# A spectral filter and a snake MLP on one core: the first DFT stage of batches 3 to 7 folded on GpSimd, and one inverse piece moved

## The chip, the cores and the metric

The kernel runs on one core of a Trainium2 chip. The metric is device time in microseconds (us) of one execution, the median over several runs; lower is better. A profiled execution of the same program gives the page and the trace that are quoted here. Its own time is not the median of the runs, and both are given below.

The engines are named as the profile names them: PE (TensorE, matrix products; PEld is its weight load), DVE (VectorE), ACT (ScalarE), POOL (GpSimd) and SP (SyncE, which here does nothing but issue DMAs). Each engine takes its instructions in the order in which the program emits them.

## The reference, cut to what matters

```python
batch, seq, dim = (8, 3008, 256)             # x; filt_r, filt_i: (1505, 256)
n_tokens, d_model, d_ff = (24064, 256, 2048) # w_in (256, 2048), w_out (2048, 256), alpha (2048,)

X = np.fft.rfft(x, axis=1)
Y = X * (filt_r + 1j * filt_i)[None, :, :]
y = np.fft.irfft(Y, n=x.shape[1], axis=1)    # per batch and channel, 3008 long

h = y.reshape(8 * 3008, 256) @ w_in
s = np.sin(alpha * h)
g = h + s * s / (alpha + 1e-09)
out = g @ w_out
```

## The kernel before

**The mixing.** A length of 3008 is 47 x 64. The transform over 3008 is made in two stages of matrix products in float16: a first stage over 47 points (of its 47 frequencies 24 are enough, since the input is real), and a second over 64 points with the twiddle factors in its tables. The way back is two stages too. For batches 1 to 7 a class `Spectral` (line 164) holds the pieces of one batch:

- `load_x` (line 175, DMA issue on line 141, queue of POOL) brings one of four quarters of the batch, 94 rows of 8 x 256, and casts it to float16.
- `first` (line 178) is one of 16 pieces of the first stage: one product of a 94 x 96 table `wf_t` with 512 columns (line 181) into a PSUM tile of the pool `fps`, which has two buffers, and a copy of it to `t1_h` by `evac`. After every fourth piece SP issues a store of the quarter to a DRAM tile `d1` (line 186).
- `load_t2` (line 189, DMA on line 193, POOL's queue) reads `d1` back with other axes on the partitions, in four groups `g` of two DMAs. It waits for the stores of `d1`.
- `forward` (line 196, products on line 201), `product` (line 211) and `cross` (line 219) make the second stage and multiply by the filter; line 208 swaps two halves of the partitions by DMA through SP. There are 12 pieces `u`; piece `u` needs group `u // 3` of `load_t2`.
- `inverse` (line 224, products on line 232) is the way back over 64 points, 12 pieces; every third piece SP stores a group to a DRAM tile `d2` (line 239). `load_t4` (line 242, SP) reads it back, and `last` (line 247, products on line 254) is the way back over 47 points, 16 pieces, into `y`.

Batch 0 has a path of its own (lines 267 to 507) ahead of the main loop and is not touched by the change, except for where two of its tiles are allocated.

**The MLP.** The 24064 columns of `y` are cut into 48 chunks, twelve for two batches: eleven of 512 columns and one of 384. `hidden` (line 534) makes one block of 128 hidden units for a chunk: two products of 512 columns (line 541) into one of four PSUM tiles, a sine on ACT (line 545) and the snake's sum on DVE (line 546), which leaves its mark in `marks["snake"]`. `project` (line 550) makes half of the second product for 128 columns: eight products of 256 columns (line 558); ACT copies two results at a time (line 566) and `store` (line 576) writes them out, from chunk 5 on through SP alone (line 586), in up to eight DMAs of a group.

**The order.** `tc.manual_schedule()` keeps the order in which the program emits. The main loop (line 640) runs in steps, eight to a chunk. A step emits two `hidden` (four products of 512), then the mixing pieces that are due (`slot(step)`), then one `project` of the chunk before (eight products of 256), then what is due by `slot(step + 0.5)`. What is due when is written out by hand in lines 602 to 623: `put(at, fn, ...)` gives a piece its step. `z = 48 * b` is where a batch's own chunks begin. `slot` emits at most one piece that has products (`pe=True`) in each half step, unless it is over a step late; a piece that has to stay behind holds back all that is due after it.

**`evac`** (line 157) gives two of three copies out of PSUM to ACT and one to DVE, in turn.

**A wait written out**: `after(ins, marks["snake"])` in `load_x` (line 152) lets a load start only when the last snake sum emitted so far is done.

Of the kernel before, what the change touches and what calls it, by code (L numbers as in the profile page):

```python
# [9 lines left out]
FP16 = mybir.dt.float16  # L10
FP32 = mybir.dt.float32
# [11 lines left out]
NR = 2 * N1  # L23
NK = 4 * NS
FUSED = 1


def dft_tables():

    n1, n2 = np.arange(N1), np.arange(N2)  # L30
    s, q = np.arange(NS), np.arange(NQ)
    ph = 2 * np.pi * np.outer(n1, s) / N1
    w = np.stack([np.cos(ph), -np.sin(ph)], 1)
    wf = np.zeros((N1, 2, 2, NS, 2))
# [12 lines left out]
    d[0, :, :, 0] = c.transpose(0, 2, 1)  # L47
    d[1, :, :, 0] = sn.transpose(0, 2, 1)
    d[0, :, :, 1] = (-sn * sg).transpose(0, 2, 1)
    d[1, :, :, 1] = (c * sg).transpose(0, 2, 1)  # L50
    f16 = np.float16
    wf, wi = wf.reshape(N1 * 2, 2, NS, 2), 2 * wi.reshape(2, NS, 2, NR)
    wf0, wi0 = np.zeros((96, 2, 2, 32)), np.zeros((2, 2, 32, NR))
    wf0[:NR, :, :, :NS] = wf.transpose(0, 1, 3, 2)
    wi0[:, :, :NS] = wi.transpose(0, 2, 1, 3)
    d = d.reshape(128, NS, 128).astype(f16)
    e = d.transpose(2, 1, 0) * f16(0.125)
    return (wf.reshape(NR, NK).astype(f16), wi.reshape(NK, NR).astype(f16), d,
            wf0.reshape(96, 128).astype(f16), wi0.reshape(128, NR).astype(f16), e)


# [1 line left out]
def kernel(  # L63
# [8 lines left out]
    out: bass.AP,  # L72
):
    nc = tc.nc
    wf_host, wi_host, d_host, wf0_host, wi0_host, e_host = dft_tables()
    wf_dram = nc.inline_tensor(wf_host, name="wf_tbl")
    wi_dram = nc.inline_tensor(wi_host, name="wi_tbl")
    d_dram = nc.inline_tensor(d_host, name="d_tbl")
    wf0_dram = nc.inline_tensor(wf0_host, name="wf0_tbl")
    wi0_dram = nc.inline_tensor(wi0_host, name="wi0_tbl")  # L80
# [13 lines left out]
        return ctx.enter_context(tc.tile_pool(name=name, bufs=bufs, **kw))  # L94

    cpool = pool("consts", 1)
    xpool = pool("xp", 4)
    t2pool = pool("t2", 4)
    xfpool = pool("xf", 3)
    ppool = pool("pp", 4)  # L100
# [19 lines left out]
    y = cpool.tile([128, 2, 2, 32, NR], FP16)  # L120
# [15 lines left out]
    marks = {}  # L136

    def load_x(b, ch):
        xt = xpool.tile([NR, 8, C], FP16, name=f"x_{b}_{ch}", tag="x")
        for n0, n in [(0, 8)] if b or ch < 3 else [(0, 4), (4, 4)]:  # L140
            ins = nc.gpsimd.dma_start(  # L141
                out=xt[:, n0:n0 + n],
                in_=bass.AP(tensor=x.tensor, offset=x.offset + (b * S + ch * 8 + n0) * C,
                            ap=[[32 * C, NR], [C, n], [1, C]]),
            )
        if b == 0:
            marks["x", ch] = ins
        if b == 1:
            marks["x1", ch] = ins
            after(ins, marks["w_out"])  # L150
        if b > 1:
            after(ins, marks["snake"])
        return xt
# [3 lines left out]
    def evac(dst, src, on_act=None):  # L157
# [3 lines left out]
        else:  # L161
            marks["dve"] = nc.vector.tensor_copy(out=dst, in_=src)  # L162

    class Spectral:

        def __init__(self, b):
            self.b = b
            self.d1 = dpool.tile([2 * NS, N2, C], FP16, name=f"d1_{b}", tag="d1")
            self.d2 = dpool.tile([2 * NS, N2, C], FP16, name=f"d2_{b}", tag="d2")
            self.d1_rows = self.d1.rearrange("a (h n) c -> (a h) n c", h=2)  # L170
            self.d2_rows = self.d2.rearrange("a (h n) c -> (a h) n c", h=2)
            self.x, self.t2, self.t4, self.xf, self.xs, self.p = {}, {}, {}, {}, {}, {}
            self.fused = b >= FUSED

        def load_x(self, ch):
# [2 lines left out]
        def first(self, i):  # L178
            ch, j = divmod(i, 4)
            ps = fps.tile([128, 512], FP32, name=f"pa_{self.b}_{i}", tag="f")  # L180
            marks["pe"] = nc.tensor.matmul(out=ps[0:NK, :], lhsT=wf_t, rhs=self.x[ch][:, 2 * j:2 * j + 2, :],  # L181
                                           start=True, stop=True)
            r0 = 8 * (ch % 2)
            evac(t1_h[ch // 2][0:NK, r0 + 2 * j:r0 + 2 * j + 2, :], ps[0:NK, :])
            if j == 3:
                nc.sync.dma_start(out=self.d1_rows[:, 8 * ch:8 * ch + 8, :], 
                                  in_=t1_h[ch // 2][0:NK, r0:r0 + 8, :])
# [76 lines left out]
    id32 = cpool.tile([16, 16], FP32)  # L264
    nc.scalar.dma_start(out=id32, in_=id32_dram.ap())

    x0 = [xpool.tile([NR, 8, C], FP16, name="x_0_0", tag="x")] + [load_x(0, ch) for ch in range(1, 4)]
# [169 lines left out]

    def product_0(i):
        hc, w = blocks[i]
        p0[i] = xpool.tile([128, 2, 4, 128], FP16, name=f"p_0_{i}", tag="x")  # L440
        marks["products"] = nc.vector.tensor_tensor(
            out=p0[i].rearrange("p f s (k c) -> p f s k c", k=2),
            in0=xf0[i].rearrange("p s (k c) -> p s k c", k=2)[:, None].to_broadcast([128, 2, 4, 2, 64]),
            in1=filt_t[:, :, 4 * w:4 * w + 4].rearrange("p f s (k c) -> p f s k c", k=2)[..., 64 * hc:64 * hc + 64],
            op=ALU.mult)
# [148 lines left out]
    def put(at, fn, *args, pe=False):  # L594
        pending.append((at, len(pending), pe, fn, args))
# [6 lines left out]
    for b in range(1, B):  # L602
        s = s1 if b == 1 else Spectral(b)
        z = 48 * b
        if b > 1:
            for ch in range(4):
                put(22 + 4 * ch if b == 2 else z - 92 + 7 * ch, s.load_x, ch)
        for i in range(16):
            put(6.9 + 0.35 * i if b == 1 else 37 + 0.63 * i if b == 2 else z - 67 + 0.66 * i, s.first, i, pe=True)
        for g in range(4):  # L610
            put(12.5 if b == 1 else 47 if b == 2 else z - 56, s.load_t2, g)
        for u in range(12):
            inv = 23.5 + 1.25 * u if b == 1 else 59 + 2.1 * u if b == 2 else z - 40.8 + 2.3 * u
            fwd = inv - (6 if b == 1 else 6)
# [68 lines left out]
```

## Time and profile before

| | us |
|---|---|
| runs, median of 3 (lowest to highest) | 784.37 (783.44 to 784.44) |
| the profiled execution, its own time | 784.61 |
| its span, first to last instruction | 782.8 |

| engine | busy us | share of the span | instructions |
|---|---|---|---|
| PE | 771.7 | 99% | 5799 |
| DVE | 654.4 | 84% | 1165 |
| ACT | 617.0 | 79% | 1211 |
| POOL | 113.3 | 14% | 190 |

The span leaves 1.8 us of the execution's time outside the first and last instruction. An engine's busy time is the union of its instructions' times. PE overlaps its products: one of 512 columns is shown as lasting some 380 ns, but the next starts 216 to 220 ns after it, so the distance between starts, not the duration, is what a product costs. The profile's time line shows those starts. "x4" in it stands for four instructions in a row.

### The profile page before, as it was taken

Reading aid. Unit: us, or ns where it says so; the run is one execution under the profiler, and the core shown is the slowest. Engines: PE = TensorE matmul, PEld = TensorE weight load, DVE = VectorE, ACT = ScalarE, POOL = GpSimd, SP = SyncE. Lnnn points to the kernel's source line nnn. Section 1 sums busy time; section 2 is a strip of 40 time slices with the busy share of each in tenths; the row PEclk is TensorE's granted clock in tenths of the full one; section 3 lists DMA queues with packets and bytes.
Section 4 is the critical chain, followed back from the end, with each engine's and each line's share of the span. In section 5 each row is a group of like instructions: output and inputs, shape, how many; then the busy total and the mean of one; then the engine's idle time right before and its main releaser. Section 6 shows DMA issues by size and latency. Waiting matters only on the chain.

```text
span 782.8 us, 16640 instructions
## 1 busy us (share of the span) xinstructions
PE 771.7 (99%) x5799; PEld 535.3 (68%) x5799; DVE 654.4 (84%) x1165; ACT 617.0 (79%) x1211; POOL 113.3 (14%) x190
## 2 busy tenths in 40 slices
PE   8999999999999999999999999999999999999998
PEld 4757767676667766777666776767667776766666
DVE  7887997899879997899878998789977899777773
ACT  5797988888778887888878888788887887777674
POOL 6366444300020000200020000200002000000000
PEclk9999999999999999999999999999999999999999
DMA  9966676655654446645574454835456233421111
GB/s 217 269 121 165 130 161 200 150 128 118 192 143 99 121 109 188 154 119 105 133 210 105 104 122 128 227 82 129 106 157 180 66 98 80 118 62 28 41 41 54
DMA packets 86655, 100.99 MB, mean 129 GB/s; under 512 B 14896, under 2 KB 74294, under 8 KB 86572
## 3 DMA queue, kind: packets, MB, share of 16 engines
q1 hardware_dynamic: 74644, 71.11, 32.6%
q0 software_dynamic: 11712, 28.78, 18.7%
q8 instruction: 45, 0.74, 0.4%
q14 instruction: 38, 0.31, 0.2%
q10 hardware_dynamic: 216, 0.05, 0.0%
HBM read 55.72 MB, written 46.66 MB: 131 GB/s over the span
## 4 chain that ended last, share of the span: by engine, by line
PE 93%; DVE 2%; POOL 1%; ACT 1%; DMA 1%; issue 1%; SPq 0%; ACTq 0%; POOLq 0%; DVEq 0%
PE po L558 41%; PE ph L541 40%; PE pa L181 3%; PE pd L254 2%; PE pb L201 2%; PE pc L232 2%; POOL w L514 1%; PE pc L453 1%; DMA al<-in_moe_alpha_dram 1%; DVE v L546 1%; PE warm L377 1%; PE pb L431 1%; SPq L586 0%; POOL w L482 0%; PE pa L399 0%
## 5 line engine op out<-in xcount | busy, mean ns | idle before, releaser
L546 DVE SCALAR_TENSOR_TENSOR v<-cos_all,ph 128x512 f16<-128x512 f32 (+1 forms) x768 | 483.2, 672 | 108.3 <-ACT cos_all L545 104.3
L545 ACT ACTIVATE cos_all<-ph 128x512 f32<-128x512 f32 (+1 forms) x768 | 411.4, 592 | 95.6 <-PE ph L541 94.7
L541 PE MATMUL ph<-y,w 128*128 128x512 f16 (+1 forms) x1536 | 388.0, 374 | 1.5 <-DVE y L162 0.8
L558 PE MATMUL po<-w,v 128*128 128x256 f16 x3008 | 389.5, 272 | 0.0
L558 PEld LDWEIGHTS <-v 128*128 128x128 f16 x3008 | 288.3, 98 | 77.8 <-issue 1.5
L541 PEld LDWEIGHTS <-w 128*128 128x128 f16 x1536 | 147.9, 98 | 104.3 <-issue 3.8
L566 ACT COPY o<-po 128x512 f32<-128x512 f32 (+1 forms) x97 | 55.7, 574 | 20.6 <-PE po L558 14.0
L586 POOL DMA_DIRECT2D out_dram<-o x67 | 35.0, 530 | 206.4 <-ACT o L566 206.2
L193 POOL DMA_DIRECT2D t<-d x56 | 36.4, 662 | 171.0 <-DMA out_dram<-o 163.6
L204 ACT CAST xf<-pb 128x512 f16<-128x512 f32 x84 | 50.0, 595 | 12.6 <-PE pb L201 11.2
L141 POOL DMA_DIRECT2D x<-in_x_dram x32 | 17.2, 540 | 269.1 <-PE pc L232 159.9
L160 ACT CAST t_h<-pa 96x512 f16<-96x512 f32 x75 | 43.9, 585 | 9.0 <-PE pa L181 8.7
L160 ACT CAST y<-pd 128x376 f16<-128x376 f32 (+1 forms) x83 | 39.9, 481 | 8.1 <-PE pd L254 4.4
L254 PEld LDWEIGHTS <-t_a 96*128 96x128 f16 x448 | 31.4, 97 | 18.6 <-issue 0.4
L181 PE MATMUL pa<-x,wf_t 94*96 94x512 f16 x112 | 42.4, 381 | 0.9 <-ACT t_h L160 0.4
L160 ACT CAST g<-pc 128x512 f16<-128x512 f32 x59 | 35.1, 594 | 7.5 <-PE pc L232 7.2
L222 DVE TENSOR_TENSOR p<-p,xs 128x512 f16<-128x512 f16 x84 | 35.7, 425 | 2.9
L254 PE MATMUL pd<-wi_t,t_a 96*128 96x94 f16 x448 | 37.1, 204 | 0.0
L221 DVE TENSOR_TENSOR xs<-xs,filt_t 128x512 f16<-128x512 f16 x84 | 35.3, 420 | 0.2 <-DMA xs<-xf 0.2
L215 DVE TENSOR_TENSOR p<-xf,filt_t 128x512 f16<-128x512 f16 x84 | 35.2, 419 | 0.0
L201 PE MATMUL pb<-t,d_t 128*128 128x256 f16 x168 | 32.0, 272 | 0.1
L232 PE MATMUL pc<-p,e_t 128*128 128x256 f16 x168 | 32.1, 273 | 0.0
(64 smaller groups left out, 284.1 us busy)
## 6 DMA issues: line engine op xcount, KB each, us to landing
x<-in_x_dram POOLq DMA_DIRECT2D x30, 376.0 KB, 4.9
d<-t_h SPq DMA_DIRECT2D x28, 384.0 KB
t<-d POOLq DMA_DIRECT2D x56, 192.0 KB, 4.3
xs<-xf SPq DMA_DIRECT2D x168, 64.0 KB
d<-g SPq DMA_DIRECT2D x56, 192.0 KB
t_a<-d SPq DMA_DIRECT2D x28, 384.0 KB
out_dram<-o SPq DMA_DIRECT2D x92, 80.0 KB
w_out<-in_moe_w_out_dram SPq DMA_DIRECT2D x2, 1024.0 KB
```

Of the source, the lines that this page charges most:

```text
L160: marks["act"] = nc.scalar.copy(out=dst, in_=src)
L181: marks["pe"] = nc.tensor.matmul(out=ps[0:NK, :], lhsT=wf_t, rhs=self.x[ch][:, 2 * j:2 * j + 2, :], start=True, stop=True)
L193: nc.gpsimd.dma_start(out=self.t2[g][64 * p:64 * p + 64, :, :], in_=self.d1[a0:a0 + 6, :, :].rearrange("s n c -> n s c"))
L201: nc.tensor.matmul(out=ps[:, i, :], lhsT=d_t[:, s, :], rhs=self.t2[s // 6][:, s % 6, :], start=True, stop=True)
L204: nc.scalar.copy(out=self.xf[u], in_=ps)
L232: nc.tensor.matmul(out=ps[:, i, :], lhsT=e_t[:, 2 * w + i, :], rhs=pt[:, i, :], start=(k == 0), stop=(k == len(pr) - 1))
L254: nc.tensor.matmul(out=psv[:, i, :], rhs=wi_t, start=True, stop=True, lhsT=t4_h[ch // 2][0:NK, n0 % 16 + i, cb * 128:cb * 128 + 128])
L541: nc.tensor.matmul(out=ps[:, 0:n], lhsT=w1[:, cb, jb * 128:jb * 128 + 128], rhs=y_cols[:, cb, c0:c0 + n], start=(cb == 0), stop=(cb == 1))
L545: nc.scalar.activation(out=cs[:, 0:n], in_=ps[:, 0:n], func=AFT.Sin, bias=float(np.pi / 2))
L546: marks["snake"] = nc.vector.scalar_tensor_tensor(out=v[k][:, jb, 0:n], in0=cs[:, 0:n], scalar=-1.0, in1=ps[:, 0:n], op0=ALU.add, op1=ALU. ...
L558: nc.tensor.matmul(out=pso[k][:, t % 2, :], lhsT=v[k][:, jb, 128 * t:128 * t + 128], rhs=w2[:, jb, :], start=(jb == 0), stop=(jb == 15))
L566: nc.scalar.copy(out=o[:, i0:t % 2 + 1, :], in_=pso[k][:, i0:t % 2 + 1, :])
```

## The change

For batches 3 to 7 the first stage is done another way. The 47 points of the first transform are taken in pairs n and 47 - n: with the sum and the difference of a pair, the cosine part needs only the sums and the sine part only the differences, so 24 rows each stand in for 47. The 64 places of the other axis, with one dummy place ahead of them, are cut in 5 runs of 13; the 5 runs lie side by side on the partitions, so that 5 x 24 = 120 partitions are used. `load_mirror` loads the rows n (`k = 0`) and the rows 47 - n (`k = 1`) for two of the 13 places at a time (the last time one), in 14 loads and one more for the rows n = 0, where `load_x` made four. `fold` makes the sums into one of four small tiles and the differences in place, two GpSimd operations on 120 x 512 (the last 120 x 256), each pair of them waiting for the last snake sum. `first_folded` is one product of a 120 x 120 table with 512 columns, `k = 0` with the sums and `k = 1` with the differences: 12 products of 512 columns and two of 256 columns for a batch in place of 16 of 512. The stores to `d1` are four, of 8 and then 5 of the 13 places, one each for the two parts. The table `wp_t` is one more load through SP at the start, ahead of those of `w_out`.

Due times in steps, for batch b with z = 48 b (before -> after):

| piece | before | after, b = 3 | after, b = 4 to 7 |
|---|---|---|---|
| loads of x | z - 92 to z - 71 | z - 92 to z - 75.1 | the same |
| folds (GpSimd) | none | z - 64.9 to z - 56.8 | z - 65.9 to z - 57.8 |
| first-stage products | z - 67 to z - 57.1 | z - 61.5 to z - 52.7 | z - 62.5 to z - 53.7 |
| `load_t2` | z - 56 | z - 51.5 | z - 52 |
| `forward`, first piece | z - 46.8 | z - 46.8 | z - 46.8 |
| `inverse`, piece 11 | z - 15.5 | z - 14.6 | z - 14.6 |

The last row holds for batch 2 too, with its own step: 82.1 before, 83 after. The tiles of x are cut from one tile `x_all` in place of a pool of four, and the two `t1_h` from one tile `t1_a`; the order in which they are used is the same. A clearing of 13 x 256 numbers on 128 partitions (`start_folding`) is added once on GpSimd at step 50.

```diff
+FOLDED = 3
+NJ, NL = 5, 13
+NF = NJ * NS
 def dft_tables():
...
-    return (wf.reshape(NR, NK).astype(f16), wi.reshape(NK, NR).astype(f16), d,
+    even = np.cos(ph[:NS])
+    odd = -np.sin(ph[:NS])
+    wp = np.einsum("kis,jm->jiksm", np.stack([even, odd]), np.eye(NJ))
+    wp = np.concatenate([wp[:, 1:].reshape(NF - NJ, 2, NF), wp[:, 0].reshape(NJ, 2, NF)])
+    return (wp.astype(f16), wf.reshape(NR, NK).astype(f16), wi.reshape(NK, NR).astype(f16), d,
...
+    wp_host, wf_host, wi_host, d_host, wf0_host, wi0_host, e_host = dft_tables()
+    wp_dram = nc.inline_tensor(wp_host, name="wp_tbl")
...
-    t1_h = [cpool.tile([128, 16, C], FP16, name=f"t1_h{i}") for i in range(2)]
+    t1_a = cpool.tile([128, 2, 16, C], FP16)
+    t1_h = [t1_a[:, i] for i in range(2)]
+    wp_t = cpool.tile([NF, 2, NF], FP16)
+    x_all = cpool.tile([128, 4, 8, C], FP16)
+    x_made = []
+    def x_tile():
+        x_made.append(x_all[:, len(x_made) % 4])
+        return x_made[-1]
...
+    STORES = {3: 0, 6: 8}
+    NP = (NL + 1) // 2
+    x_rows = x_all.rearrange("p a n c -> p (a n) c")
+    mirror = [x_rows[:, 16 * k:16 * k + NL, :] for k in range(2)]
+    sums = [t[0:NF, NL:NL + 2, :] for t in (t1_h[0], t1_h[1], x_rows[:, 0:16], x_rows[:, 16:32])]
+
+    def start_folding():
+
+        nc.gpsimd.memset(mirror[1].bitcast(UINT32), 0)
+
     class Spectral:
         def __init__(self, b):
             self.b = b
-            self.d1 = dpool.tile([2 * NS, N2, C], FP16, name=f"d1_{b}", tag="d1")
+            self.folded = b >= FOLDED
+            if self.folded:
+                self.d1_all = dpool.tile([2 * NS, NJ * NL, C], FP16, name=f"d1_{b}", tag="d1f")
+                self.d1 = self.d1_all[:, 1:1 + N2, :]
+                self.d1_fold = self.d1_all.rearrange("(k s) (j l) c -> k (s j) l c", k=2, j=NJ)
+            else:
+                self.d1 = dpool.tile([2 * NS, N2, C], FP16, name=f"d1_{b}", tag="d1")
+                self.d1_rows = self.d1.rearrange("a (h n) c -> (a h) n c", h=2)
             self.d2 = dpool.tile([2 * NS, N2, C], FP16, name=f"d2_{b}", tag="d2")
-            self.d1_rows = self.d1.rearrange("a (h n) c -> (a h) n c", h=2)
             self.d2_rows = self.d2.rearrange("a (h n) c -> (a h) n c", h=2)
-            self.x, self.t2, self.t4, self.xf, self.xs, self.p = {}, {}, {}, {}, {}, {}
+            self.e, self.x, self.t2, self.t4, self.xf, self.xs, self.p = {}, {}, {}, {}, {}, {}, {}
             self.fused = b >= FUSED
         def load_x(self, ch):
...
+
+        def load_mirror(self, k, l0, n):
+            rows = [mirror[k][0:NF - NJ, l0:l0 + n]] + ([] if k or l0 else [mirror[k][NF - NJ:NF]])
+            for at, t in zip((N2 * (N1 - 1) if k else N2, 0), rows):
+                run = n if at else NL
+                ins = nc.gpsimd.dma_start(
+                    out=t, in_=bass.AP(tensor=x.tensor, offset=x.offset + (self.b * S + at - 1 + l0) * C,
+                                       ap=[[NL * C, NJ], [-N2 * C if k else N2 * C, NS - 1 if at else 1],
+                                           [1, run * C]]))
+                after(ins, marks["snake"])
+
+        def fold(self, i):
+            l0, n = 2 * i, min(2, NL - 2 * i)
+            xa, xb = [t[0:NF, l0:l0 + n, :] for t in mirror]
+            self.e[i] = sums[i % 4]
+            after(nc.gpsimd.tensor_tensor(out=self.e[i][:, 0:n, :], in0=xa, in1=xb, op=ALU.add), marks["snake"])
+            nc.gpsimd.tensor_tensor(out=xa, in0=xa, in1=xb, op=ALU.subtract)
+
+        def first_folded(self, i, k):
+            l0, n = 2 * i, min(2, NL - 2 * i)
+            if n == 2 or k == 0:
+                self.ps1 = fps.tile([128, 2, C], FP32, name=f"pa_{self.b}_{i}_{k}", tag="f")
+            ps = self.ps1
+            if k == 0:
+                src = self.e[i][:, 0:n, :]
+            else:
+                src = mirror[0][0:NF, l0:l0 + n, :]
+            dst = ps[0:NF, 0:2, :] if n == 2 else ps[0:NF, k:k + 1, :]
+            nc.tensor.matmul(out=dst, lhsT=wp_t[:, k, :], rhs=src, start=True, stop=True)
+            if n == 2:
+                evac(t1_a[0:NF, k, l0:l0 + 2, :], ps[0:NF])
+            elif k == 1:
+                evac(t1_a[0:NF, :, l0, :], ps[0:NF])
+            if i in STORES and k == 1:
+                lo = STORES[i]
+                n = l0 + n - lo
+                for part in range(2):
+                    nc.sync.dma_start(out=self.d1_fold[part, :, lo:lo + n, :], in_=t1_a[0:NF, part, lo:lo + n, :])
...
     nc.sync.dma_start(out=wi_t, in_=wi_dram.ap())
+    nc.sync.dma_start(out=wp_t, in_=wp_dram.ap())
     w_out32 = vpool.tile([128, 16, C], FP32, name="w_out32", tag="v")
...
     for b in range(1, B):
         s = s1 if b == 1 else Spectral(b)
         z = 48 * b
-        if b > 1:
-            for ch in range(4):
-                put(22 + 4 * ch if b == 2 else z - 92 + 7 * ch, s.load_x, ch)
-        for i in range(16):
-            put(6.9 + 0.35 * i if b == 1 else 37 + 0.63 * i if b == 2 else z - 67 + 0.66 * i, s.first, i, pe=True)
+        if s.folded:
+            if b == FOLDED:
+                put(z - 94, start_folding)
+            for i in range(NP):
+                for k in range(2):
+                    put(z - 92 + 2.6 * i + 1.3 * k, s.load_mirror, k, 2 * i, min(2, NL - 2 * i))
+            for i in range(NP):
+                at = z - (61.5 if b == 3 else 62.5) + 1.35 * i
+                put(at - 3.4, s.fold, i)
+                for k in range(2):
+                    put(at + 0.7 * k, s.first_folded, i, k, pe=True)
+        else:
+            if b > 1:
+                for ch in range(4):
+                    put(22 + 4 * ch, s.load_x, ch)
+            for i in range(16):
+                put(6.9 + 0.35 * i if b == 1 else 37 + 0.63 * i, s.first, i, pe=True)
         for g in range(4):
-            put(12.5 if b == 1 else 47 if b == 2 else z - 56, s.load_t2, g)
+            put(12.5 if b == 1 else 47 if b == 2 else z - (51.5 if b == 3 else 52), s.load_t2, g)
         for u in range(12):
             inv = 23.5 + 1.25 * u if b == 1 else 59 + 2.1 * u if b == 2 else z - 40.8 + 2.3 * u
             fwd = inv - (6 if b == 1 else 6)
...
-            put(inv, s.inverse, u, pe=True)
+            put(inv + (0.9 if b > 1 and u == 11 else 0), s.inverse, u, pe=True)
```

More of the change, by code (lines that the diff above doesn't have):

```diff
@@ L74 @@
     nc = tc.nc
-    wf_host, wi_host, d_host, wf0_host, wi0_host, e_host = dft_tables()
+    wp_host, wf_host, wi_host, d_host, wf0_host, wi0_host, e_host = dft_tables()
     wf_dram = nc.inline_tensor(wf_host, name="wf_tbl")
     wi_dram = nc.inline_tensor(wi_host, name="wi_tbl")
+    wp_dram = nc.inline_tensor(wp_host, name="wp_tbl")
     d_dram = nc.inline_tensor(d_host, name="d_tbl")
@@ L96 @@
     cpool = pool("consts", 1)
-    xpool = pool("xp", 4)
     t2pool = pool("t2", 4)
@@ L138, in load_x @@
     def load_x(b, ch):
-        xt = xpool.tile([NR, 8, C], FP16, name=f"x_{b}_{ch}", tag="x")
+        xt = x_tile()[0:NR]
         for n0, n in [(0, 8)] if b or ch < 3 else [(0, 4), (4, 4)]:
@@ L265 @@
     nc.scalar.dma_start(out=id32, in_=id32_dram.ap())
-    x0 = [xpool.tile([NR, 8, C], FP16, name="x_0_0", tag="x")] + [load_x(0, ch) for ch in range(1, 4)]
+    x0 = [x_tile()[0:NR]] + [load_x(0, ch) for ch in range(1, 4)]
     nc.gpsimd.dma_start(out=d_t, in_=d_dram.ap())
@@ L439, in product_0 @@
         hc, w = blocks[i]
-        p0[i] = xpool.tile([128, 2, 4, 128], FP16, name=f"p_0_{i}", tag="x")
+        p0[i] = x_tile()[:, 0:4].rearrange("p n (f c) -> p (n f) c", f=2).rearrange("p (f s) c -> p f s c", f=2)
         marks["products"] = nc.vector.tensor_tensor(
```

## The prediction

> **What bounds the kernel now.** I read the page first, then PE by stretches, PE's time line about one first stage, groups by line and shape, and the queues of SP and POOL. From the page:
>
> ```profile
> PE 771.7 (99%) x5799; PEld 535.3 (68%) x5799; DVE 654.4 (84%) x1165; ACT 617.0 (79%) x1211; POOL 113.3 (14%) x190
> ...
> PE 93%; DVE 2%; POOL 1%; ACT 1%; DMA 1%; issue 1%; SPq 0%; ACTq 0%; POOLq 0%; DVEq 0%
> ```
>
> The second line is the chain that ended last: nearly all of it is PE. Busy PE could still be slow PE, so I looked at the distance between starts on the time line of PE about the first stage of batch 4 (columns: start and duration in us, engine, line, operation, how many in a row):
>
> ```profile
> 302.66 0.38 PE L181 MATMUL pa<-x,wf_t 94*96 94x512 f16 x1
> 302.88 1.04 PE L558 MATMUL po<-w,v 128*128 128x256 f16 x8
> 303.75 0.38 PE L181 MATMUL pa<-x,wf_t 94*96 94x512 f16 x1
> 303.97 1.03 PE L541 MATMUL ph<-y,w 128*128 128x512 f16 x4
> 304.84 0.38 PE L181 MATMUL pa<-x,wf_t 94*96 94x512 f16 x1
> ...
> 310.67 0.33 PE L254 MATMUL pd<-wi_t,t_a 96*128 96x94 f16 x4
> ...
> 321.74 0.38 PE L201 MATMUL pb<-t,d_t 128*128 128x256 f16 x2
> ```
>
> A first-stage product takes 302.88 - 302.66 = 0.22 us of PE, eight products of 256 columns (303.75 - 302.88) / 8 = 0.109 each, four of 512 columns (304.84 - 303.97) / 4 = 0.217. So the cost goes by columns. Summed over all starts from 80 us on, what goes beyond these distances is 1.7 us in 700: PE waits for nothing there. A column saved is time saved, and anything that makes PE wait costs in full, since no idle time is there to take it up.
>
> **What is removed from PE.** Per batch, 16 products at 0.22 = 3.52 us. Added: 12 of 512 columns at 0.22 = 2.64 and two of 256 at 0.11 = 0.22, in all 2.86. The table has 120 columns where the old one has 96; the old weight load shows 123 ns, the 128-column ones 98, and neither shows between starts even behind a 0.109 us product, so I count the new one at nothing. Saved: 0.66 us a batch, **3.3 us** for five. The three copies out of PSUM saved per batch (ACT and DVE, 0.6 to 0.7 us each) are hidden by PE and count as nothing. Waits of the old pieces for their PSUM copies (0.9 us idle before line 181, all batches together) may go: up to 0.4 more, taken as 0.
>
> **The folds on POOL.** No row shows a float16 sum on POOL. The nearest ones, in the groups by line and shape (busy us in all, mean ns of one, idle time ahead):
>
> ```profile
> L482 POOL TENSOR_TENSOR w<-w_in,y 128x512 f16<-128x512 f32 x2 | 2.6, 1276 | 0.0
> ...
> L285 POOL TENSOR_TENSOR rest<-al,part 16x128 f32<-16x128 f32 x1 | 0.4, 419 | 0.1
> ```
>
> The first has 512 numbers per partition and two inputs: 1.28 us. The second, 128 numbers with one bfloat16 input, is 0.42; four of them, start-up paid four times, give an upper end of 1.68. As a lower end, the row of 768 numbers (1837 ns) against 512 gives 2.2 ns a number with no start-up: 1.12. I take 1.28, a pair 2.55. Due times leave 1.35 steps from pair to pair; the old stage ran at 21.1 us for 9.9 steps (283.73 to 304.84), 2.1 us a step, so some 2.0 with 0.66 us less in it, and a pair has 2.7 us. The first product is due 3.4 steps = 6.8 us after its fold, of which the wait for the snake sum takes up to 1.5. The last full pair's difference is ready at 1.5 + 12 p and needed at 6.8 + 5 x 2.7 + 0.7 x 2.0 = 21.7, so PE first waits at **p = 1.68 us** an operation. At 1.28 the slack is 4.8 us: cost 0. At the upper end it is used up, cost still 0. If that cover goes, every further 0.1 us costs 12 x 0.1 x 5 batches = 6 us. The two waits per pair hold up only the next folds: POOL's next other work is `load_t2`, 5.8 steps after the last fold. The clearing at step 50 and 55 more loads at about 0.54 us (line 141) lie on an engine 14% busy, 17 steps or more ahead of the folds that need them.
>
> Do sums on POOL slow DVE? In the stretch from 37.8 to 49.9 us POOL ran its operations of lines 482 and 514 with only loads between:
>
> ```profile
> L546 DVE SCALAR_TENSOR_TENSOR v<-cos_all,ph 128x512 f16<-128x512 f32 x16 | 9.8, 683 | 1.3 <-ACT cos_all L545 1.3
> ```
>
> 683 ns is also the mean of all 704: no slowing, cost 0. The Trainium skill, "SBUF — State Buffer", section "SBUF: two separate sides", speaks against the change: a GpSimd operation and a VectorE one with two SBUF inputs lock each other out for a whole instruction. Line 546 has one input in PSUM, and lines 215, 221 and 222, with two in SBUF, never meet a sum on POOL here, so the trace doesn't test it. By that page the last `cross` of the batch before, two instructions, could each lose one fold, an estimate of 2 x 1.28 us of DVE per batch, 12.8 in all, and if all of it reached PE the sum would end at about 795 us.
>
> **The later start of the second stage** is the dangerous part. `forward` stays at z - 46.8 while the last first-stage product moves from z - 57.1 to z - 53.7 (b = 3: z - 52.7). By the steps in the time line, the new place for batch 4 is behind the eight products that end at 310.67, 11.1 us ahead of 321.74 (before: 16.9). Counted in the same way: 11.1 for batches 3 and 6, 13.1 for 5 and 7. What has to fit, from SP and POOL in batch 4:
>
> ```profile
> 301.75 1.64 SPq L244 DMA_DIRECT2D t_a<-d  x3
> 307.23 0.30 SPq L186 DMA_DIRECT2D d<-t_h  x1
> 307.62 7.95 SPq L586 DMA_DIRECT2D out_dram<-o  x11
> ...
> 311.50 5.19 POOL L193 DMA_DIRECT2D t<-d  x8 [32.28 <-DMA out_dram<-o]
> ```
>
> From the last product's start to SP's store: 307.23 - 304.84 = 2.4 us here, 1.3 to 2.4 over batches 3 to 7, mean 1.8. From the store to the first `load_t2` on POOL: 311.50 - 307.23 = 4.3 here; 5.4, 5.3, 4.8 and 5.6 in the others, all with three `t_a` loads of 384 KB just ahead in the same queue; in batch 2, without them, at most 4.1, POOL being busy with output stores until then. From there to the landing of the first group's second load: 3.9 to 4.4, mean 4.2. The new last store is two DMAs of 5 x 120 rows, 614 KB against 393: at the 269 GB/s of the page's second slice 0.8 us more, and 0.36 for the second issue. The `t_a` loads are now some 6 us ahead, so I start from 4.1. Chain: 1.8 + 4.1 + 0.8 + 0.4 + 4.2 = **11.3 us** against 11.1; lowest 1.3 + 4.1 + 3.9 = 9.3 (a bigger store no slower), highest 2.4 + 5.6 + 1.2 + 4.4 = 13.6. Late by 0.2 by the means; as an early batch wins nothing back, I take 0.3 in each of batches 3, 4 and 6, 0 in the others: **0.9 us**, between 0 and 3 x 2.5 + 2 x 0.5 = 8.5. Queued behind a late `forward` on PE is everything, `hidden` and `project` too.
>
> **The rest.** Piece 11 of `inverse` issues two products, a copy and two `d2` stores 0.9 steps later, past part of an output group on SP; `load_t4` at z - 10.5 waits for the stores on SP, 4.1 steps = 7.8 us after the product, against 2.4 for the copy, 1.3 for two issues and 2.6 to 3.0 to land (the output stores on POOL): 6.7 at most, so no wait. In batch 2 only 2.5 steps are left, and SP may stand for 1.5 us; late next would be `last`, 4 steps on: 0. The load of `wp_t` (57.6 KB, 0.2 us at 269 GB/s) stands ahead of `w_out`, which POOL's first x load waits for and which the chain passes at 40 to 50 us (line 514): +0.2, between 0 and 0.6 with its issue, 0.38 like the table's before it.
>
> **Sum**: -3.3 + 0.9 + 0.2 = -2.2 us. The profiled execution, 784.61 with a span of 782.8 and 1.8 around it, would go to a span of 780.6. Its time is 0.2 above the median of the runs, 784.37, which goes to **782.2**. Its own range: -3.3 - 0.4 = 780.7 to -3.3 + 2.1 (0.7 late in three batches) + 0.6 = 783.8.
>
> **Rivals.**
> - *The second stage comes late (other side).* Place: `forward` of group 0 behind store and load. PE loses (c - 11.1) in three batches and (c - 13.1) in two; against 3.1 saved it decides from c = 11.1 + 3.1 / 3 = 12.1 us. At the top, c = 13.6, -3.3 + 8.5 + 0.2 gives 789.8. For it: 2.4 us to SP and five output issues near that place. Against: the queue is clear of `t_a` loads.
> - *It lands within reach of no change*: c about 11.7 to 12.4, so that 1.7 to 3.9 us are given back; 784.1.
> - *The folds are the bound*: from p = 1.68; at 2.0 us, 12 x 0.32 x 5 = 19 us, 800.4. For it: no float16 row. Against: 1.28 for the nearest.
> - *The columns are saved, but DVE or ACT sets the pace*: 784.4. Against: PE's 1.7 us of waits with DVE at 84%, and three copies fewer a batch.
>
> **Numbers.** Forecast 0.63, late second stage 0.14, no change by it 0.15, folds 0.04, DVE or ACT 0.04. Told apart from no change is 0.2%, 1.6 us: faster 0.63, same 0.19, slower 0.18. Likeliest **782.2**; the range from 780.5 to 786.5 takes in the forecast's own, the case of no change and half of the late one.
>
> **What would show it.** Right: starts of first-stage products 0.22 us apart from the next, PE idle only ahead of `forward` of batches 3, 4 and 6, each under 1 us, folds at 1.2 to 1.4 us. Wrong: idle time of PE at the new products that POOL ended (folds), at `forward` that a DMA ended in all batches, or line 546 longer than 683 ns beside the folds.

## The result, and the profile after

| | before | after |
|---|---|---|
| runs, median (lowest to highest), us | 784.37 (783.44 to 785.30, 9 runs) | 786.56 (785.05 to 788.92, 9 runs) |
| the profiled execution, us | 784.61 | 785.86 |
| its span, us | 782.8 | 784.0 |
| PE at the pace of its columns, us | 760.8 | 757.6 |
| PE's waits up to 80 us, us | 14.8 | 15.4 |
| PE's waits from 80 us on, us | 1.7 | 5.7 |

After against before is 1.0024, with a 95% interval from 1.0014 to 1.0034: slower, where faster was forecast. The last three rows are worked out as in the prediction, from the distances between starts on PE; what goes beyond the columns' pace is a wait. They split the 1.25 us between the two profiled executions: 3.2 less for the columns, 3.9 more for waits in the main part, 0.6 more at the start. The medians lie 2.2 us apart; the other 0.9 belongs to runs without a trace.

From the page of the kernel after, engine by engine, and the chain that ended last:

```profile
PE 771.0 (98%) x5789; PEld 533.1 (68%) x5789; DVE 657.2 (84%) x1160; ACT 613.3 (78%) x1201; POOL 228.4 (29%) x316
...
PE 89%; DMA 4%; DVE 3%; POOL 2%; ACT 1%; issue 1%; SPq 0%; POOLq 0%; DVEq 0%; ACTq 0%
```

PE has 10 products less, but its share of the chain falls from 93 to 89%, in favour of DMA, DVE and POOL. Nearly all that POOL gains, and over half of what DMA gains, lies ahead of 80 us, where the chain takes another way through the loads of the start. From 80 us on it passes over DMA for 15.0 us (2.1 before) and over DVE for 17.2 (3.7 before): swaps `xs`, `load_t2`, the two operations of `cross` and snake sums. DVE is busy for 2.8 us more, though it was rid of copies out of PSUM. The groups by line and shape (busy us in all, mean ns of one, idle ahead) say which operations grew:

```profile
L618 DVE SCALAR_TENSOR_TENSOR v<-cos_all,ph 128x512 f16<-128x512 f32 x704 | 449.6, 682 | 89.4 <-ACT cos_all L617 84.7 <-POOL w L586 1.7
...
L293 DVE TENSOR_TENSOR p<-p,xs 128x512 f16<-128x512 f16 x84 | 39.9, 475 | 2.9
L292 DVE TENSOR_TENSOR xs<-xs,filt_t 128x512 f16<-128x512 f16 x84 | 38.1, 453 | 1.8 <-DMA xs<-xf 1.8
...
L286 DVE TENSOR_TENSOR p<-xf,filt_t 128x512 f16<-128x512 f16 x84 | 35.0, 417 | 0.0
L237 POOL TENSOR_TENSOR x_all<-x_all 120x512 f16<-120x512 f16 x30 | 35.0, 1165 | 2.4
...
L236 POOL TENSOR_TENSOR t_a<-x_all 120x512 f16<-120x512 f16 x20 | 23.8, 1188 | 87.7 <-DVE v L618 87.4
```

The folds (lines 236 and 237) take 1.17 us. The snake sum (line 618, before 546) is as it was: the 80 of its 704 that ran beside a fold have a mean of 681 ns, the others 682. The two operations of `cross` (lines 292 and 293, before 221 and 222) are not. Before they were

```profile
L222 DVE TENSOR_TENSOR p<-p,xs 128x512 f16<-128x512 f16 x84 | 35.7, 425 | 2.9
L221 DVE TENSOR_TENSOR xs<-xs,filt_t 128x512 f16<-128x512 f16 x84 | 35.3, 420 | 0.2 <-DMA xs<-xf 0.2
```

Times of DVE and then of POOL in the kernel after, ahead of batch 5's first stage (start and duration in us), show that the means hide one slow pair in each of batches 3 to 7:

```profile
378.35 0.42 DVE L292 TENSOR_TENSOR xs<-xs,filt_t 128x512 f16<-128x512 f16 x1
378.80 0.42 DVE L293 TENSOR_TENSOR p<-p,xs 128x512 f16<-128x512 f16 x1
...
382.13 1.04 DVE L292 TENSOR_TENSOR xs<-xs,filt_t 128x512 f16<-128x512 f16 x1
383.21 1.26 DVE L293 TENSOR_TENSOR p<-p,xs 128x512 f16<-128x512 f16 x1
```

```profile
380.51 1.15 POOL L236 TENSOR_TENSOR t_a<-x_all 120x512 f16<-120x512 f16 x1 [16.75 <-DVE v L618]
381.74 1.16 POOL L237 TENSOR_TENSOR x_all<-x_all 120x512 f16<-120x512 f16 x1
382.85 1.33 POOL L236 TENSOR_TENSOR t_a<-x_all 120x512 f16<-120x512 f16 x1
384.26 1.22 POOL L237 TENSOR_TENSOR x_all<-x_all 120x512 f16<-120x512 f16 x1
```

Line 292 starts at 382.13, while the fold that began at 381.74 is running, and takes 1.04 us in place of 0.42. Line 293 starts inside the next fold and ends at 384.47, 0.29 after that fold. The two folds that meet them are longer too, 1.33 and 1.22 in place of 1.15. The two kinds of operation run by turns. In the whole trace 10 of the 168 operations of `cross` meet a fold, two a batch. All ten are slow (line 292 takes 0.63 to 1.14 us, line 293 1.26), and none of the other 158 is over 0.43. I call this the lock. What sets the slow operations apart from the snake sums and copies beside the same folds is that both their inputs lie in SBUF, but they are also of another kind, all float16; no run changes the place of an input alone. DVE loses 0.62 + 0.84 = 1.5 us there, and just behind it PE stands (PE's time line, the same place):

```profile
384.79 0.38 PE L303 MATMUL pc<-p,e_t 128*128 128x256 f16 x2
385.12 1.19 PE L613 MATMUL ph<-y,w 128*128 128x512 f16 x4
386.14 0.38 PE L249 MATMUL pa<-t_a,wp_t 120*120 120x512 f16 x1
```

Two products of 256 columns last until the next start at 385.12, 0.33 us where 0.22 is their pace, and four of 512 take 1.02 in place of 0.87: 0.28 us of waits for the snake sums queued behind the slow cross. The same pair stands in all five batches and costs DVE 7.1 us in all.

The second thing that grew is the way of `load_t2`. From the page, DMA issues (KB each, median us from issue to landing), before and then after:

```profile
t<-d POOLq DMA_DIRECT2D x56, 192.0 KB, 4.3
```

```profile
t<-d POOLq DMA_DIRECT2D x56, 192.0 KB, 5.8
```

What is new among PE's waits from 80 us on ("where" is the start of the product ahead of the wait):

| what PE waits for | where | us |
|---|---|---|
| snake sums and a copy behind the slow cross | 293.5, 294.0, 384.9, 385.3, 479.8, 480.2, 482.0, 571.6, 572.1 | 1.53 |
| first stage of batch 3, a copy on DVE behind the slow cross | 201.6 | 0.59 |
| `load_t2` at the first `forward` | batch 2: 0.66, batch 3: 0.26 | 0.92 |
| `inverse`, 5 to 6 us after a `cross` stood for a swap `xs` (0.5 and 1.3 us) | 274.3, 460.5 | 0.58 |
| one piece of `inverse`, its `p` from `cross`; in the variants too, but for those with longer loads | 287.7, 565.8 | 0.31 |

They sum to 3.93, as much as 5.67 - 1.74. Some smaller waits, of 0.2 us each at most, came or went besides (two for copies, at 203.5 and 381.7 us before, are gone; one at 309 us is new) and nearly cancel.

### The profile page after: what moved, and what is told of

It is laid out like the page before. It is cut to its first block, busy times and chain, and to the rows that moved or that the text cites. A ratio compares the mean times of both kernels' runs of the same rounds, so it can differ in the third digit from the quotient of the medians.

```text
span 784.0 us, 16831 instructions
## 1 busy us (share of the span) xinstructions
PE 771.0 (98%) x5789; PEld 533.1 (68%) x5789; DVE 657.2 (84%) x1160; ACT 613.3 (78%) x1201; POOL 228.4 (29%) x316
## 3 DMA queue, kind: packets, MB, share of 16 engines
q0 software_dynamic: 36512, 28.97, 22.0%
## 4 chain that ended last, share of the span: by engine, by line
PE 89%; DMA 4%; DVE 3%; POOL 2%; ACT 1%; issue 1%; SPq 0%; POOLq 0%; DVEq 0%; ACTq 0%
PE po L630 39%; PE ph L613 38%; PE pb L272 2%; PE pd L325 2%; PE pc L303 2%; PE pa L249 2%; DVE v L618 1%; DMA id<-id 1%; DMA xs<-xf 1%; DMA w_out<-in_moe_w_out_dram 1%; PE pa L214 1%; POOL w L586 1%; PE pb L502 1%; POOL x_all L158 0%; DMA t<-d 0%
## 5 line engine op out<-in xcount | busy, mean ns | idle before, releaser
L226 POOL DMA_DIRECT2D x_all<-in_x_dram x75 | 47.5, 635 | 155.3 <-DVE v L618 149.2
L638 ACT COPY o<-po 128x512 f32<-128x512 f32 (+1 forms) x97 | 55.7, 574 | 18.9 <-PE po L630 11.9
L236 POOL TENSOR_TENSOR t_a<-x_all 120x512 f16<-120x512 f16 x20 | 23.8, 1188 | 87.7 <-DVE v L618 87.4
L177 ACT CAST t_a<-pa 120x512 f16<-120x512 f32 (+1 forms) x64 | 37.8, 590 | 13.9 <-PE pa L249 8.7
L293 DVE TENSOR_TENSOR p<-p,xs 128x512 f16<-128x512 f16 x84 | 39.9, 475 | 2.9
L292 DVE TENSOR_TENSOR xs<-xs,filt_t 128x512 f16<-128x512 f16 x84 | 38.1, 453 | 1.8 <-DMA xs<-xf 1.8
L237 POOL TENSOR_TENSOR x_all<-x_all 120x512 f16<-120x512 f16 (+1 forms) x35 | 38.3, 1094 | 2.7
```

Of the source, the lines that this page charges most:

```text
L177: marks["act"] = nc.scalar.copy(out=dst, in_=src)
L226: ins = nc.gpsimd.dma_start(out=t, in_=bass.AP(tensor=x.tensor, offset=x.offset + (self.b * S + at - 1 + l0) * C, ap=[[NL * C, NJ], [-N2 * ...
L237: nc.gpsimd.tensor_tensor(out=xa, in0=xa, in1=xb, op=ALU.subtract)
L293: nc.vector.tensor_tensor(out=p, in0=p, in1=xs, op=ALU.add)
L638: nc.scalar.copy(out=o[:, i0:t % 2 + 1, :], in_=pso[k][:, i0:t % 2 + 1, :])
```

## The experiments

Each edit is made on the kernel after, except for the last one. "PE's waits" are those from 80 us on in its profile.

| kernel | median, us | against before (95%) | profiled, us | PE's waits, us |
|---|---|---|---|---|
| after | 786.56 | 1.0024 (1.0014 to 1.0034) | 785.86 | 5.7 |
| e1_late_folds | 787.78 | 1.0030 (1.0019 to 1.0041) | 787.78 | 6.4 |
| e2_wp_last | 785.03 | 1.0010 (0.9999 to 1.0022) | 784.40 | 5.7 |
| e3_t4_later | 786.07 | 1.0012 (1.0003 to 1.0020) | 784.47 | 4.5 |
| e4_early_folds | 788.96 | 1.0047 (1.0033 to 1.0062) | 788.22 | 8.8 |
| e5_folds_after_cross | 786.76 | 1.0017 (1.0006 to 1.0029) | 784.52 | 5.5 |
| e6_all_three | 784.41 | 0.9997 (0.9988 to 1.0005) | 785.49 | 5.4 |
| e7_wp_and_t4 | 786.49 | 1.0020 (1.0011 to 1.0030) | 786.22 | 5.7 |
| e8_piece11_back | 792.57 | 1.0094 (1.0081 to 1.0107) | 790.47 | 11.7 |
| e9_long_loads | 816.46 | 1.0394 (1.0366 to 1.0422) | 817.00 | 38.2 |
| e10_four_edits | 784.04 | 0.9987 (0.9977 to 0.9996) | 783.46 | 3.6 |
| e11_five_edits | 815.10 | 1.0387 (1.0368 to 1.0407) | 818.01 | 37.5 |
| e12_before_piece11 | 785.66 | 1.0008 (0.9999 to 1.0017) | 784.14 | 2.0 |

The kernel before stood at 784.56 beside the first four experiments, 785.01 beside the next four and 784.97 beside the last four, so the ratios are what is compared.

### Folds later

```diff
-                put(at - 3.4, s.fold, i)
+                put(at - 1.6, s.fold, i)
-            after(nc.gpsimd.tensor_tensor(..., op=ALU.add), marks["snake"])
+            after(nc.gpsimd.tensor_tensor(..., op=ALU.add), marks["pace"])
```

`marks["pace"]` is the last snake sum or cross emitted.

> The folds are due 1.6 steps ahead of their products in place of 3.4, and each waits for the last cross as well as for the last snake sum, so that no fold runs beside a cross. Theory L (lock: the second fold pair runs beside the last cross of the batch before, whose two instructions then last 1.1 and 1.26 us in place of 0.42 each, and PE waits behind them; some 2.2 us of waits in the profile of the changed kernel): no cross above 0.45 us, and the time falls by 1.5 to 2.5 us, to 784.0 to 785.1. Theory T (the load of the second stage is late because the last quarter of the t_a loads runs beside it): nothing changes, 786.0 to 787.2. Theory S (the new table's load delays the start): nothing changes.

Of theory L's forecast, one half came. No cross is over 0.43 us any more, and the waits behind it are gone. But PE now waits for the folds, up to 1.15 us in batch 3. The group of the first products with a sum in it, by shape:

```profile
L249 PE MATMUL pa<-t_a,wp_t 120*120 120x512 f16 x20 | 7.7, 384 | 1.3 <-POOL t_a L236 1.0
```

1.6 steps are too short a lead, and the time didn't fall. The edit took away one wait and made another, so it doesn't price the lock.

### Folds earlier

The same line with `at - 5.0`, the old wait.

> The folds are due 5.0 steps ahead of their products in place of 3.4, so that they run beside two crosses of the batch before in place of one. Theory L: twice as many slow cross instructions (some 20 in place of 10) and 1 to 3 us more, 787.5 to 789.5. Theories T and S: no change, 786.0 to 787.2.

Theory L held, with fewer slow operations than it said. DVE in batch 4's turn, in this kernel:

```profile
285.61 1.01 DVE L286 TENSOR_TENSOR p<-xf,filt_t 128x512 f16<-128x512 f16 x1
...
291.41 1.14 DVE L292 TENSOR_TENSOR xs<-xs,filt_t 128x512 f16<-128x512 f16 x1
292.59 1.26 DVE L293 TENSOR_TENSOR p<-p,xs 128x512 f16<-128x512 f16 x1
```

Two or three operations a batch with both inputs in SBUF are slow now, the filter product of line 286 among them, 14 in all over 1 us where some 20 were expected, and PE's waits rise by 3.1 us to 8.8. At 287.8, 379.9, 475.0 and 567.6 PE waits 0.55 to 0.75 us for a `p` that is late, which it didn't before. With the same work at an earlier place the ratio goes from 1.0024 to 1.0047; the two intervals just touch.

### Folds just after the cross

```diff
-                put(at - 3.4, s.fold, i)
+                put(at - (1.85 if b == 3 else 2.4), s.fold, i)
-            after(nc.gpsimd.tensor_tensor(..., op=ALU.add), marks["snake"])
+            ins = nc.gpsimd.tensor_tensor(..., op=ALU.add)
+            if i == 0:
+                after(ins, marks["cross"])
```

> The folds start 2.4 steps ahead of their products (3.4 before; 1.85 for batch 3), the first one waits for the sum of the last cross emitted, the others wait for no snake sum. The lead is between that of e1_late_folds (1.6, folds late) and that of the changed kernel. Theory L (lock between a fold and a cross): no cross operation over 0.5 us, no PE wait on POOL, and the waits of some 0.3 us just after the cross in batches 3 to 7 gone, 2.2 us in all: profiled time about 783.7, PE waits from 80 us on about 3.5 in place of 5.7. Rival F (the folds can't be put anywhere without PE paying for them): new waits of PE on POOL at the first-stage products, as in e1_late_folds, and no gain. Rival T (only the late t2 loads matter): the waits at forward stay and the time moves by less than 0.5.

DVE and POOL at the place shown above for the kernel after:

```profile
382.23 0.42 DVE L294 TENSOR_TENSOR xs<-xs,filt_t 128x512 f16<-128x512 f16 x1
382.68 0.43 DVE L295 TENSOR_TENSOR p<-p,xs 128x512 f16<-128x512 f16 x1
383.03 2.67 DVE L620 SCALAR_TENSOR_TENSOR v<-cos_all,ph 128x512 f16<-128x512 f32 x4
```

```profile
383.20 1.15 POOL L236 TENSOR_TENSOR t_a<-x_all 120x512 f16<-120x512 f16 x1 [19.34 <-DVE p L295]
384.43 1.15 POOL L239 TENSOR_TENSOR x_all<-x_all 120x512 f16<-120x512 f16 x1
385.54 1.16 POOL L236 TENSOR_TENSOR t_a<-x_all 120x512 f16<-120x512 f16 x1
```

The cross is back at 0.42, the folds at 1.15, and the folds beside the snake sums (line 620) slow nobody. In batches 4 to 7 not one wait behind the cross is left, and none for a fold. The sum of 3.5 us of waits didn't come, though (5.5), and neither did the time (1.0017, where 1.0024 can't be told from it): batch 3, with its own lead of 1.85 steps, waits 1.16 us for its first fold in place of 0.59, and waits for `load_t2` (1.1 us) and for a late swap (0.87) are larger in this profile. The fall of the lock is shown here, its price is not.

### The last quarter of `load_t4` later, the table last

```diff
-            put(z - (9.5 if b == 1 and ch < 3 else (10.5, 10.5, 10.5, 3)[ch]), s.load_t4, ch)
+            put(z - (9.5 if b == 1 and ch < 3 else (10.5, 10.5, 10.5, 3 if b == 1 else -3)[ch]), s.load_t4, ch)
```

> The last quarter of load_t4 of batches 2 to 7 is due at z + 3 in place of z - 3; the pieces that need it are due from z + 15. Theory T: the first pair of load_t2 of batches 4 to 7 lands 3.3 to 4.2 us after its issue as before (5.3 to 7.0 in the changed kernel), and the time falls by 0.5 to 1.5 us with a narrower spread of the runs (3.9 us from lowest to highest in the changed kernel, 1.9 before). Theories L and S: 786.3 to 786.9, spread as it was.

SP and then POOL in the kernel after, at `load_t2` of batch 5:

```profile
408.47 0.32 SPq L315 DMA_DIRECT2D t_a<-d  x1
```

```profile
408.41 5.28 POOL L264 DMA_DIRECT2D t<-d  x8 [10.38 <-DMA d<-t_a]
```

A load of 384 KB and eight of 192 KB start within 0.06 us of each other in two queues. The second load of the first group lands at 415.32, with `forward` at 416.95. With the quarter six steps later it lands at 411.78, with `forward` at 415.87, and the page of that kernel has

```profile
t<-d POOLq DMA_DIRECT2D x56, 192.0 KB, 4.5
```

The wait for these loads in batch 3 is gone, and the slack in batches 4 to 7, from 0.4 to 1.6 us after, is 2.4 to 4.1. So it was this quarter that had brought the second stage to its edge. What this does to the time isn't shown: the ratio, 1.0012, has an interval that overlaps that of the kernel after, and with `wp_t` moved as well it is 1.0020.

The other edit moves the load of `wp_t` behind those of `w_out` on SP.

> The load of the table wp_t stands behind the two of w_out in place of ahead of them. Theory S: the first x load of batch 1 on POOL starts at about 37.2 us as before (37.8 in the changed kernel) and the time falls by 0.4 to 0.7 us, to about 786.0. Theories L and T: nothing changes beyond 0.2 us.

The profile was faster by 1.5 us, all of it ahead of 80 us, as theory S would have it. That doesn't show the term: the first x load of batch 1 on POOL, which stands at 37.19 us before and 37.84 after, was at 36.34 here, but at 37.78 and 38.12 in the two later kernels with the same edit, and at 35.71 and 36.35 in two (e5, e8) without it. In e12, whose program up to there is that of the kernel before, it was at 36.33. The start scatters by 2.4 us for reasons that no run here tells, and an effect of this table of some tenths can't be seen in it.

> wp_t last and the last quarter of load_t4 later, the folds as in the changed kernel. Sum of the two: about -2.4, median about 784.2, so no difference from the kernel before; the cross operations at 1.04 and 1.26 us stay. The distance to e6_all_three is the price of the lock alone: 1.5 to 2.5 us by theory L, 0 if the lock is hidden.

Both edits and the old folds: 1.0020, 786.49 where 784.2 was expected, no gain that can be told from the kernel after; the slow crosses are all there (lines 292 and 293 at a mean of 454 and 474 ns).

> The edits of e5_folds_after_cross, e2_wp_last and e3_t4_later together. If the three causes are separate and add up: -2.2 (lock) -1.2 (start) -1.0 (t2 loads) from the profiled 785.86, so about 781.5 profiled, median about 782.2, PE waits from 80 us on 2.0 to 2.5: faster than the kernel before by 2 us. If they hide each other, between 783 and 784.5.

With the folds moved as well the ratio is 0.9997. The two kernels ran on the same chip in turns and differ in the folds alone: 1.0020 (from 1.0011) against 0.9997 (to 1.0005), 2.1 us between the medians. The intervals don't meet, so with the two other edits in place the move of the folds gains time. How much of that is the lock is less sure than the expectation had it. The waits behind the slow cross in the kernel after, 1.53 + 0.59 = 2.1 us, are as large as the gain, but the move also makes new waits: in the two profiles PE's waits differ by only 0.4 us (5.7 and 5.4), and made on the kernel after alone (e5) the same move can't be told from nothing. So 2.1 us is the lock's price by the waits in one profile; the runs show a gain in one pair of kernels and none in the other. e6 was not faster than before by the 2 us hoped for: three waits were left, 1.05 us for `load_t2` of batch 2, 1.16 for the first fold of batch 3 and 1.1 for late swaps.

### Piece 11 back

```diff
-            put(inv + (0.9 if b > 1 and u == 11 else 0), s.inverse, u, pe=True)
+            put(inv + 0, s.inverse, u, pe=True)
```

> Piece 11 of inverse back at its old step, the rest as in the changed kernel. By theory L the 0.9 steps (1.8 us) are what covers the crosses slowed by the folds: without them PE waits for p at that piece in batches 2 to 6, 0.5 to 1.5 us each, 3 to 6 us in all, about 790. By the prediction, which costed the move at nothing and saw no lock: no change, 786 to 787.

792.57: the wait stands at the place that theory L names. PE's time line before batch 5's first stage:

```profile
383.48 1.04 PE L630 MATMUL po<-w,v 128*128 128x256 f16 x8
385.82 0.39 PE L303 MATMUL pc<-p,e_t 128*128 128x256 f16 x2 [1.31 <-DVE p L293]
```

Eight products should give way after 0.87 us and do so after 2.34: a wait of 1.47 for `p` of the slow cross. The five such waits are 0.97, 1.54, 1.47, 1.48 and 1.54, in all 7.0 us, more than the 3 to 6 expected and about what DVE loses to the lock (7.1). So the lock would have cost that; the 0.9 steps hide about two thirds of it.

> The kernel before with nothing changed but piece 11 of inverse 0.9 steps later in batches 2 to 7. By the prediction the move costs nothing: same as before within 0.5 us. Rival: the move itself costs, by a load_t4 that starts later on SP: 0.3 to 1 us slower, with PE waits ahead of last.

The move by itself, in the kernel before, is 1.0008, and the interval touches 1. The one new wait in its profile that is over 0.05 us, 0.29 at 213.6 for a load of `t_a`, is of the rival's kind. The move costs little or nothing where there is no lock.

### Longer loads

```diff
-            for i in range(NP):
+            for i in range(2):
                 for k in range(2):
-                    put(z - 92 + 2.6 * i + 1.3 * k, s.load_mirror, k, 2 * i, min(2, NL - 2 * i))
+                    put(z - 92 + 10 * i + 5 * k, s.load_mirror, k, 6 * i, 6 + i)
```

> The mirrored rows are loaded 6 or 7 of the 13 places at a time, four loads and one small one a batch in place of 14 and one; the rest as in the changed kernel. Theory X (the many loads with short runs make the xs swaps land late, so that a cross and behind it PE waits: 0.2 to 0.9 us at piece places of batches 3 and 5): packets of the software queue fall to well under half, DVE idle ahead of the cross on xs falls from 1.8 to 0.2 us as in the kernel before, PE waits from 80 us on fall by 0.4 to 0.8. If only the number of bytes counts: no change. The late t2 loads and the lock stay in either case.

Packets of the software queue fell from 36,512 to 17,312, and the time rose by 4%: theory X has it the wrong way round. The groups in this kernel of the second cross operand and of the inverse products by shape:

```profile
L292 DVE TENSOR_TENSOR xs<-xs,filt_t 128x512 f16<-128x512 f16 x84 | 38.5, 458 | 30.1 <-DMA xs<-xf 30.1
...
L303 PE MATMUL pc<-p,e_t 128*128 128x256 f16 x168 | 32.6, 277 | 21.2 <-DVE p L293 21.2
```

DVE stands 30.1 us for the swaps (1.8 after), PE behind it. A long load is 10.6 us from issue to landing, a short one 5.3. Why it is so much worse than `load_x`, 376 KB and 4.9 us in the kernel before, wasn't tried.

### The version that is left

Folds as in e5 for batches 4 to 7 and as in the kernel after for batch 3, `load_t4` as in e3, and

```diff
-                put(6.9 + 0.35 * i if b == 1 else 37 + 0.63 * i, s.first, i, pe=True)
+                put(6.9 + 0.35 * i if b == 1 else 36.5 + 0.63 * i, s.first, i, pe=True)
```

> Folds after the cross for batches 4 to 7 (lead 2.4 steps, one wait for the cross) and as in the changed kernel for batch 3; the last quarter of load_t4 six steps later for batches 2 on; the first stage of batch 2 half a step earlier. From e6_all_three's PE waits from 80 us on of 5.35 us: less 1.05 (forward of batch 2 late) and 0.57 (folds of batch 3 late, 1.16 against 0.59), so about 3.7; the start, which varied by 1.5 us between profiles whatever the edit, left out. Median about 783.2, 1.5 below the kernel before. If such waits come back elsewhere, 784.5 as e6_all_three.

3.6 us of waits, as expected, and 784.04 against 784.97: 0.9987 (0.9977 to 0.9996), 0.9 us less where 1.5 was expected. It beats the kernel before by 0.13%, and its interval lies below that of the kernel after. By the profile's sums it should be -3.2 + (3.6 - 1.7) = -1.3 us; the medians give -0.9. With the long loads added it falls behind as e9 did (1.0387):

> e10_four_edits with the long loads of e9_long_loads. If theory X holds, about 0.7 below e10_four_edits, median 782.5; else the same as e10_four_edits.

## Why the prediction was wrong

**Right: the columns.** The forecast was 3.3 us less on PE; it was 3.2. Of the 60 new products of 512 columns 50 start 0.22 us before the next, the others 0.24 or 0.26, which is 0.2 us in all; more than that the wider table can't have cost.

**Right: the folds as a bound.** 1.17 us each, between the ends 1.12 and 1.68 and nearer the lower one than the 1.28 taken. PE waits for no fold at a lead of 3.4 steps.

**The step that failed: "Do sums on POOL slow DVE? ... no slowing, cost 0".** The row that it rested on, line 546 beside the operations of POOL, has an input in PSUM; that row is unchanged after (682 ns). The two-SBUF-input rows were named there as never meeting a sum on POOL, and still took the price of the other row. The rule that speaks against it stood in the prediction with an estimate, 795 us, but got no term in the sum, no rival and no chance. The new due times were at hand: the last `cross` of a batch, in the next batch's z, is due at z - 65.0, and the first folds at z - 65.9 and z - 64.55. By these times one fold pair meets one cross. The Trainium skill, "SBUF — State Buffer", section "SBUF: two separate sides", says that a GpSimd operation and a VectorE one with both inputs in SBUF lock each other out for the length of an instruction, if the GpSimd one reads SBUF, as the folds do. The trace after agrees: 0.42 becomes 1.04 and 1.26 us, while the sums with an input in PSUM are untouched (681 ns beside a fold). Its estimate in the prediction, two folds of DVE a batch or 12.8 us in all, is above what the runs show: 7.1 us of DVE in all, or 1.4 a batch (two folds, each less what was already over), 7.0 us of PE with no cover (e8), 2.1 with the moved piece as a cover, by the waits in the profile. None of the three signs of being wrong that the prediction named came: PE waited for no fold, the wait at `forward` is in batches 2 and 3 only, and the snake sum kept its 682 ns. They watched the row that doesn't feel the folds.

**"Piece 11 ... 0" was right as a price and wrong as a reading.** The step saw a move that costs nothing. It didn't ask what the move was covering: without it, 1.5 steps lie between the last cross and its product, too few for a cross that is 1.5 us late. Undone, the ratio goes from 1.0024 to 1.0094.

**The late second stage: the sum right by luck, its parts not.** Forecast 11.3 us from the last product to the landing of the second load; measured 10.5, 10.8, 11.5, 10.6 and 11.9, mean 11.1. Store and issue were shorter than forecast (from the first of the last two stores to `load_t2` 3.0 to 3.3 us, where 4.1 + 0.8 + 0.4 was taken), the landing longer (5.2 to 7.7 against 4.2), since the last quarter of `load_t4`, due at z - 3, now runs beside it. The prediction had seen the three `t_a` loads go out of the way, and not that the fourth came into it. The two errors cancelled. Waits in batches 3 to 7: 0.26 us against 0.9 taken, all in batch 3, where the products left 10.4 us and not the 11.1 counted (219.35 to 229.70 in e3, where PE doesn't wait there). In batch 2 there are 0.66 more that no step had: its store, unchanged in size, is 4.8 us from `load_t2` where it was 4.1 (4.4 to 5.3 in all profiles of the new kernel and its variants, 4.1 in e12). Why is open; half a step earlier for its first stage removes the wait (e10) and makes some 0.3 us of others at the earlier products.

**The start: 0.2 forecast, 0.6 in the one profile,** inside a scatter of 2.4 us of the start; not told apart.

**Late swaps, 0.6 us,** had no step. Loads of x run beside them in the other queue; e9 shows that larger loads make them far worse, and no run shows that the short ones are their cause. The 0.3 us of the one piece of `inverse` had no step either and stay open.

So -2.2 became +1.3 in the profile by the lock (2.1), the swaps (0.6), `load_t2` of batch 2 (0.7) and the start (0.4 over the 0.2 forecast), the piece of `inverse` (0.3) and 0.1 of the columns, less 0.6 that the late stage didn't take; the parts are rounded and come to 1.4. Of the 4.4 us between the forecast and the median, 0.9 lie in runs without a trace and stay open.

## What to carry to other kernels

Work put on an idle GpSimd isn't free for VectorE: look for each VectorE operation with both inputs in SBUF that will run beside it by the new due times, and price it at the rest of the running GpSimd operation. A neighbour with an input in PSUM is no evidence: here its 682 ns stayed while 0.42 us became 1.26. Where a change also moves a piece by a little, ask what wait the move covers, for its price is then the price of that wait. And a stage that is put later takes a new set of neighbours in the DMA queues: list those that it leaves and those that it meets.

## What the runs showed of the hardware

- A float16 sum of 120x512 on GpSimd takes 1.15 us, 0.13 less than the float32 row of 128x512 beside which it was estimated. Beside a float16 VectorE operation with both inputs in SBUF the two take turns (1.04 and 1.26 us for 0.42; 1.33 and 1.22 for 1.15). The VectorE sum with one input in PSUM isn't slowed: 681 ns for 80 of them beside such sums, 682 for the others.
- One load of 384 KB from SP, issued within 0.06 us of eight of 192 KB from POOL, makes the first two of these land 2.5 to 2.7 us later (batch 5: 6.2 and 6.9 us after the first issue, against 3.5 and 4.4 with that load out of the way).
- Where mirrored loads of up to 402.5 KB (10.6 us to land) take the place of loads of 115 KB (5.3 us) for the same bytes, VectorE stands 30.1 us in all for the 64 KB swaps in the other queue, against 1.8. How the one delays the other isn't shown.
